# Narrow zero-weight filler matmuls and a scheduler that models tile switches, in a two-layer attention kernel

## The chip, the cores and the metric

The kernel runs on one core of one Trainium2 chip. The metric is the device time of one execution in microseconds. Most executions agree within 0.3%.

In this text ScalarE is ACT, VectorE is DVE and TensorE is PE (PEld for its weight loads) in the profile's lines.

## The reference

Two layers, each of them a multi-query attention (A) followed by a linear attention (B), over 2048 tokens of width 512. A has 32 query heads of width 16 and one head of keys and values:

```python
def _A_ref(x, wq, wk, wv, wo):                       # cut
    q = (x @ wq).reshape(B, S, 32, 16).transpose(0, 2, 1, 3)
    k = x @ wk
    v = x @ wv
    p = softmax(einsum("bhqd,bkd->bhqk", q, k) * 16 ** -0.5)
    o = einsum("bhqk,bkd->bhqd", p, v)
    return o.transpose(0, 2, 1, 3).reshape(B, S, 512) @ wo
...
x = A_x
x = x + A(layernorm(x)); x = x + B(layernorm(x))     # layer 1
x = x + A(layernorm(x)); x = x + B(layernorm(x))     # layer 2
```

What matters is the softmax: 2 x 32 x 2048 x 2048 exponentials. In tiles of 128 keys x 512 (queries, or queries of several heads) these are 4096 score tiles, 2048 for each layer.

## The kernel before

The kernel plans itself. While it is being built, a list scheduler written in Python walks through a model of the engines, with a duration for each operation, and fixes the order of instructions on every engine. On the chip that order is kept, and only semaphores decide when an instruction starts.

A score tile goes one of two ways. ScalarE takes them in threes: three score matmuls, then one exp of 128x1536. VectorE takes them in pairs, with a polynomial in six steps. TensorE then multiplies the tile with the values. Scores use 32 rows of the array (three matmuls in different row groups run side by side), values use 32 columns (four column groups, side by side). Both write to PSUM (TensorE's output memory, eight banks here), of which VectorE's scores and, in the attention stages, all projections share one bank, number 6.

```python
# scores: row group i of 32 rows          (smm, cut)
x = e.matmul(bank(b0 + k), lhsT=Kr[r, m, kt * P:(kt + 1) * P], rhs=QT[r, ..., q0:q0 + n], start=True, stop=True)
# values: column group c of 32 columns    (add_pv, cut)
return e.matmul(ps[32 * c:32 * c + 32, 7 * 512:8 * 512], lhsT=Vaug[:, kt, :], rhs=src, ...)
o = add(PE, 0.1, f, ..., name="pv")
# a projection: four matmuls in two operations of two (proj, cut)
for c in range(0, len(mms), chunk):                  # chunk = 2
    o = add(PE, len(part) * (0.03 + n * 0.36e-3), f, ...)
```

Between these the kernel puts fillers: matmuls with zero weights, added to the bank of the values, so that they change no result. They keep TensorE active enough for its full clock. In the kernel before they use the whole array:

```python
def idle(now):                                       # called when PE has nothing in the model (cut)
    if not sc.order[PE] or streaming(now) > FILL * FILLW:       # 0.6 of the last 1.7 us
        return
    ...
    o = add(PE, 0.03 + FILLN * 0.41e-3, lambda e: e.matmul(bank(7, FILLN), lhsT=zer[:],
            rhs=maskx[:].bitcast(BF16)[:, 0:FILLN], start=not owned, stop=True, ...), prio=9.0, name="dummy")
```

The softmax here doesn't subtract the row's maximum and nothing guards it: scores larger than these inputs give would overflow.

## Time and profile before

| quantity | before |
|---|---|
| time, median | 1781.3 us in 3 runs |
| ScalarE busy | 1728.1 of 1777.9 us, 97% |
| exps (1536 columns each, but for 3 of 1024), one every | 1207, 1.331 us |
| score tiles on VectorE / on ScalarE | 478 / 3618 |
| fillers | 1234 |

The lines of the profile's page, first: span; busy time of the engines; the chain of work that ended last, by engine; then four groups of instructions (line, engine, operation, output<-input, count, busy us and mean ns of one, idle time just before them and what ended it). One record of exp covers about 1.57 us, but the next starts 1.331 us after it, since they overlap.

```profile
span 1777.9 us, 27691 instructions
...
PE 1683.0 (95%) x11642; PEld 533.4 (30%) x11642; DVE 1554.0 (87%) x2767; ACT 1728.1 (97%) x1452; POOL 31.3 (2%) x46
...
ACT 62%; PE 19%; DVE 17%; issue 1%; DMA 0%; POOL 0%; SPq 0%
...
L775 ACT ACTIVATE PTA<-ps_all 128x1536 bf16<-128x1536 f32 x1207 | 1644.0, 1569 | 7.7 <-PE ps_all L635 6.3
...
L897 PE MATMUL ps_all<-maskx,zer 128*128 128x512 bf16 x1234 | 401.0, 386 | 0.0
L829 DVE TENSOR_SCALAR xT<-ps_all 128x512 int32<-128x512 f32 x478 | 327.4, 685 | 80.8 <-PE ps_all L635 78.9
```

Three windows of 100 us in the second attention stage show where the room is. Each line has the start and end, then the busy us and (count) of PE, PEld, DVE, ACT and POOL, the clock, the DMA share and GB/s; two lines are copied, the last window and the sum of the three.

```profile
1600.00:1700.00 100.00, 95.40 (x673) 29.78 (x672) 81.57 (x147) 99.71 (x79) 2.98 (x3) 1.00 0.00 1
sum 300.00, PE 287.33 PEld 86.99 DVE 254.12 ACT 298.49 POOL 5.28; mean PE 95.78 PEld 29.00 DVE 84.71 ACT 99.50 POOL 1.76
```

ScalarE is busy 99.5% of the time there. The timeline of ScalarE shows how tight that is: 24 exps in a row in 32.40 us. From start to start they are 1.331 us apart, but for a few of 1.34 to 1.35 us and one of 1.585 us.

```profile
1098.61 32.40 ACT L775 ACTIVATE PTA<-ps_all 128x1536 bf16<-128x1536 f32 x24
```

So the kernel is a sequence of exps with little between them: 1207 x 1.331 = 1606.5 us of the span of 1777.9 us. The other 171.4 us are called "time outside exps" below. They hold the start (the ramp, before exps follow each other closely), the stretch between the layers, the end, ScalarE's other work, and waits. For waits there is a second number, the "excess": within the two attention stages, how much the distance from each exp to ScalarE's next instruction exceeds 1.331 us, summed. It is 29.3 us before; where exactly a stage is taken to begin and end moves such a sum by about 1 us. (A first version of it, over fixed stretches of time and between neighbouring exps alone, gave 28.7 us before. Some texts quote that one; the tables here use the second.)

The list of waits of VectorE (engine, what waited <- what it waited for: us in total, times, longest):

```profile
DVE xT L829 <- PE ps_all L635: 78.9, 129, 1.3
DVE e_buf L940 <- ACT e_buf L939: 45.2, 29, 2.8
DVE v_tok L958 <- PE ps_all L496: 25.3, 19, 3.1
...
DVE rden L695 <- PE ps_all L692: 2.1, 2, 1.1
```

And a microsecond and a half of TensorE's timeline: scores (line 635), values (671) and a filler (897). Merged lines carry the start of the first matmul of the group.

```profile
401.63 0.39 PE L635 MATMUL ps_all<-QT,Kr 32*128 32x512 bf16 x3
401.95 0.40 PE L671 MATMUL ps_all<-PTA,Vaug 128*32 128x512 bf16 x3
402.28 0.39 PE L897 MATMUL ps_all<-maskx,zer 128*128 128x512 bf16 x1
402.85 0.40 PE L635 MATMUL ps_all<-QT,Kr 32*128 32x512 bf16 x4 [0.18 <-ACT PTA L775]
```

From 401.63 to 401.95 (scores to values) and from 401.95 to 402.28 (values to filler), each change of kind takes 0.32 us from start to start, where two matmuls of one kind in one place take 0.216 us. (The scores at 402.85 had to wait for ScalarE besides.) A change costs about 0.1 us. The Trainium skill, "TensorEngine Tiling (Array Packing)", Key Properties, states that changing the tiling mode drains the engine; this trace agrees and puts a number to it.

### The profile page before, as it was taken

The page shows a single profiled execution, that of the slowest core. Times are in us where ns is not written, and L with a number is a line of the kernel's source. Part 1 is how long each engine was busy: PE and PEld are TensorE (multiplying, and loading weights), DVE is VectorE, ACT ScalarE, POOL GpSimd, SP SyncE. Part 2 cuts the span into 40 slices and gives each one's busy share as a digit, 9 for nine tenths or more (in the row PEclk, how much of TensorE's full clock was granted, in tenths as well). Part 3 has the DMA queues.
Part 4 walks back from the last instruction along what each step waited for, and adds up shares of the span by engine and source line. Part 5 has one row for each costly group of instructions (what it writes and reads, how often), then busy time and mean ns, then how long its engine had stood idle before and what let it go on. Part 6 is the DMA issues. An engine that isn't in the chain of part 4 may idle for free.

```text
span 1777.9 us, 27691 instructions
## 1 busy us (share of the span) xinstructions
PE 1683.0 (95%) x11642; PEld 533.4 (30%) x11642; DVE 1554.0 (87%) x2767; ACT 1728.1 (97%) x1452; POOL 31.3 (2%) x46
## 2 busy tenths in 40 slices
PE   7999999999999999999899999999999999999998
PEld 4222222222232222233442222322222322222334
DVE  7999997999887998878789999879998879978775
ACT  7999999999999999999699999999999999999996
POOL 0000000000000000000000000000000000000000
PEclk9999999999999999999999999999999999999999
DMA  3000000000000000000000000000000000000001
GB/s 120 1 1 1 1 1 1 1 1 1 1 1 1 1 1 1 1 1 1 1 1 1 1 1 1 1 1 1 1 1 1 1 1 1 1 1 1 1 1 48
DMA packets 7724, 9.14 MB, mean 5 GB/s; under 512 B 1456, under 2 KB 7088, under 8 KB 7600
## 3 DMA queue, kind: packets, MB, share of 16 engines
q1 hardware_dynamic: 7600, 7.37, 1.3%
q8 instruction: 91, 1.49, 0.3%
q14 instruction: 33, 0.27, 0.1%
HBM read 5.28 MB, written 2.10 MB: 4 GB/s over the span
## 4 chain that ended last, share of the span: by engine, by line
ACT 62%; PE 19%; DVE 17%; issue 1%; DMA 0%; POOL 0%; SPq 0%
ACT PTA L775 60%; PE ps_all L635 6%; PE ps_all L671 5%; PE ps_all L897 3%; DVE xT L829 3%; DVE PTD L851 3%; PE ps_all L496 2%; ACT e_buf L939 1%; DVE xs L847 1%; DVE xu L846 1%; DVE xs L850 1%; DVE stats L461 1%; PE ps_all L1060 1%; DVE xs L848 1%; DVE xu L849 1%
## 5 line engine op out<-in xcount | busy, mean ns | idle before, releaser
L775 ACT ACTIVATE PTA<-ps_all 128x1536 bf16<-128x1536 f32 x1207 | 1644.0, 1569 | 7.7 <-PE ps_all L635 6.3
L635 PE MATMUL ps_all<-QT,Kr 32*128 32x512 bf16 x4096 | 611.3, 385 | 39.8 <-ACT PTA L775 14.8
L671 PE MATMUL ps_all<-PTA,Vaug 128*32 128x512 bf16 x3618 | 520.1, 390 | 8.2 <-DVE Eo L683 7.8
L897 PE MATMUL ps_all<-maskx,zer 128*128 128x512 bf16 x1234 | 401.0, 386 | 0.0
L829 DVE TENSOR_SCALAR xT<-ps_all 128x512 int32<-128x512 f32 x478 | 327.4, 685 | 80.8 <-PE ps_all L635 78.9
L635 PEld LDWEIGHTS ps_all<-QT,Kr 32*128 32x128 bf16 x4096 | 147.2, 91 | 486.3 <-ACT PTA L775 188.1
L851 DVE SCALAR_TENSOR_TENSOR PTD<-xT,xs 128x1024 uint16<-128x1024 int32 x239 | 290.3, 1215 | 1.8
L671 PEld LDWEIGHTS ps_all<-PTA,Vaug 128*32 128x32 bf16 x3618 | 126.2, 93 | 319.0 <-issue 299.9
L846 DVE TENSOR_SCALAR xu<-xT 128x1024 f16<-128x1024 uint16 x239 | 164.3, 687 | 3.7
L847 DVE TENSOR_TENSOR xs<-xu 128x1024 f16<-128x1024 f16 x239 | 163.5, 684 | 2.9
L850 DVE TENSOR_TENSOR xs<-xs,xu 128x1024 f16<-128x1024 f16 x239 | 163.0, 682 | 2.4
L897 PEld LDWEIGHTS ps_all<-maskx,zer 128*128 128x128 bf16 x1234 | 93.9, 97 | 196.5 <-issue 179.4
L671 PE MATMUL ps_all<-PTD,Vaug 128*32 128x512 bf16 x478 | 128.8, 388 | 18.2 <-DVE Eo L683 11.4
L848 DVE TENSOR_SCALAR xs<-xs 128x1024 f16<-128x1024 f16 x239 | 98.9, 414 | 1.7
L849 DVE TENSOR_SCALAR xu<-xu 128x1024 f16<-128x1024 f16 x239 | 99.2, 415 | 0.0
L496 PE MATMUL ps_all<-wqkv_sb,xnT 128*128 128x512 bf16 x256 | 68.7, 382 | 1.5 <-DVE xT L829 0.9
L940 DVE TENSOR_SCALAR e_buf<-e_buf 128x512 f32<-128x512 f32 x64 | 27.1, 423 | 45.4 <-ACT e_buf L939 45.2
L469 POOL TENSOR_TENSOR rstd<-veps,mhalf 128x1 f32<-128x1 f32 x30 | 27.8, 925 | 1668.5 <-DVE veps L467 1668.5
L939 ACT ACTIVATE e_buf<-ps_all 128x512 f32<-128x512 f32 x64 | 46.0, 719 | 4.8 <-PE ps_all L496 3.1
L671 PEld LDWEIGHTS ps_all<-PTD,Vaug 128*32 128x32 bf16 x478 | 28.2, 93 | 65.2 <-DVE PTD L851 30.7
L461 DVE BATCH_NORM_STATS2 stats<-x_sb 128x6 f32<-128x512 bf16 x64 | 43.2, 680 | 3.8 <-DMA x_sb<-in_A_x_dram 2.9
L683 DVE COPY Eo<-ps_all 128x512 f32<-128x512 f32 x62 | 42.4, 684 | 4.3 <-PE ps_all L671 3.7
(87 smaller groups left out, 825.9 us busy)
## 6 DMA issues: line engine op xcount, KB each, us to landing
out_dram<-x_sb SPq DMA_DIRECT2D x16, 128.0 KB, 1.7
x_sb<-in_A_x_dram SPq DMA_DIRECT2D x3, 512.0 KB, 6.9
wqkv_sb<-in_B_wqkv_dram SPq DMA_DIRECT2D x1, 1536.0 KB, 11.3
x_sb<-in_A_x_dram SPq DMA_DIRECT2D x2, 256.0 KB, 3.1
wq_sb<-in_A_wq_dram SPq DMA_DIRECT2D x1, 512.0 KB, 5.1
wo_sb<-in_A_wo_dram SPq DMA_DIRECT2D x1, 512.0 KB, 8.3
wo_sb<-in_B_wo_dram SPq DMA_DIRECT2D x1, 512.0 KB, 10.9
wk_sb<-in_A_wk_dram SPq DMA_DIRECT2D x1, 16.0 KB, 2.5
```

The lines of the kernel that those rows point to most:

```text
L496: i = e.matmul(bank(h.idx, n), lhsT=l, rhs=r, start=(c + k == 0), stop=(c + k == len(mms) - 1))
L635: x = e.matmul(bank(b0 + k), lhsT=Kr[r, m, kt * P:(kt + 1) * P], rhs=QT[r, self.units[u][0] % 2, gs, q0:q0 + n], start=True, stop=True)
L671: return e.matmul(ps[32 * c:32 * c + 32, 7 * 512:8 * 512], lhsT=Vaug[:, kt, :], rhs=src, start=opened[0], stop=opened[1], skip_group_check ...
L775: oe = add(AC, tac(m * 512), lambda e: e.activation(PTA[:, hp.idx, 0:m * 512], bank(3 * s, m * 512), ACTF.Exp, scale=SCALE), deps=[o] + pr ...
L829: o = add(DV, tdv(512), lambda e: e.tensor_scalar(out=xT[:, hx.idx, i * 512:(i + 1) * 512], in0=bank(6), scalar1=SCALE * LOG2E * 65536.0, ...
L846: o = add(DV, tdv(w, 0.52), lambda e: e.tensor_scalar(out=u_, in0=lo, scalar1=1.0 / 65536, scalar2=-0.5, op0=ALU.mult, op1=ALU.add), deps= ...
L847: o1 = add(DV, tdv(w, 0.52), lambda e: e.tensor_tensor(out=s_, in0=u_, in1=u_, op=ALU.mult), deps=[o] + c["prev"], name="xsq", **kw)
L848: o2 = add(DV, tdv(w, 0.26), lambda e: e.tensor_scalar(out=s_, in0=s_, scalar1=XK, scalar2=-XW, op0=ALU.mult, op1=ALU.add), deps=[o1], nam ...
L849: o3 = add(DV, tdv(w, 0.26), lambda e: e.tensor_scalar(out=u_, in0=u_, scalar1=1.0, scalar2=XL, op0=ALU.mult, op1=ALU.add), deps=[o1], nam ...
L850: o4 = add(DV, tdv(w, 0.52), lambda e: e.tensor_tensor(out=s_, in0=s_, in1=u_, op=ALU.mult), deps=[o2, o3], name="xc", **kw)
L851: o5 = add(DV, tdv(w), lambda e: e.scalar_tensor_tensor(out=PTD[:, hp.idx, 0:w].bitcast(U16), in0=xT[:, k, 0:w], scalar=2.0 ** -9, in1=s_, ...
L897: o = add(PE, 0.03 + FILLN * 0.41e-3, lambda e: e.matmul(bank(7, FILLN), lhsT=zer[:], rhs=maskx[:].bitcast(BF16)[:, 0:FILLN], start=not ow ...
```

## The change

The intent: let a filler queue behind the last value matmul, in the same mode and the same column group, so that no switch is paid and values of other column groups can run beside it. Further, tell the scheduler's model what the trace shows (a pass of 512 columns is 0.217 us, a switch 0.1 us, transposes and projections are shorter than it thought), and hold matmuls back that would run into a more urgent one. The part "no bank lent" is no edit: that option was already off.

The diff, cut to its core:

```diff
+SWITCH, PASS = 0.1, 0.217
...
+    def pe_need(self, o):                 # when may o start on PE, by kind (F full, S scores, P values)
+        k, g = o.pk
+        if k != self.pk:
+            return self.pend_t + SWITCH
+        return self.pend_t if k == "F" else max([self.pgrp.get(x, 0.0) for x in g])
...
+            if e == PE:                   # in the loop over ready operations, most urgent first
+                need = self.pe_need(o)
+                if need > self.now + 1e-9:
+                    if limit is None or need < limit:
+                        limit = need
+                        self.at(need, None)
+                    continue
+                if limit is not None and self.now + o.dur[PE] > limit + 0.03:
+                    continue              # the "reserving rule" of the text below
...
-    FILL, FILLW, FILLN = 0.6, 1.7, 512
+    AWIN, ATGT, ATGT2 = 1.7, 0.5, 0.6
...
-            o = add(PE, len(part) * (0.03 + n * 0.36e-3), f, ...)    # and eight more such durations
+            o = add(PE, len(part) * (0.006 + n * 0.42e-3), f, ...)
...
-            o = add(PE, 0.1, f, ..., name="pv")
+            o = add(PE, PASS, f, pk=("P", (c,)), ..., name="pv")
...
+            twice = not self.ramp and not owned and activity(sc.now) < ATGT2 and sc.tfree[AC] > sc.now + 3 * PASS
+                if twice:
+                    self.smm(e, got, 3 * s)          # scores computed twice, as a filler between units
...
+            c = max(range(4), key=lambda c: sc.pgrp.get(c, 0.0) if sc.pk == "P" else 0.0)
+            f = lambda e: e.matmul(ps[32 * c:32 * c + 32, 7 * 512:8 * 512], lhsT=zer[:, 0:32],
+                                   rhs=maskx[:].bitcast(BF16)[:, 0:512], start=not owned, stop=True, ...)
```

More of the change, by code (lines that the diff above doesn't have):

```diff
@@ L17 @@
 FLEX = 0.0
+SWITCH, PASS = 0.1, 0.217
 class Op:
     __slots__ = ("engs", "fn", "dur", "prio", "deps", "nleft", "succ", "rt", "guard", "acq", "uses", "rel", "cb",
-                 "eng", "t0", "vis", "idx", "gidx", "waits", "marked", "val", "vc", "dma", "done", "name")
+                 "eng", "t0", "vis", "idx", "pk", "gidx", "waits", "marked", "val", "vc", "dma", "done", "name")
 class Holder:
@@ L64, in __init__ @@
         self.idle = lambda now: None
+        self.pk, self.pgrp, self.pend_t = "F", {}, 0.0
     def add(self, engs, dur, fn, reads=(), writes=(), prio=5.0, guard=None, acq=(), uses=(), rel=(), cb=None, deps=(),
-            dma=False, name=""):
+            dma=False, name="", pk=("F", ())):
         o = Op()
+        o.pk = pk
         o.engs = engs if isinstance(engs, tuple) else (engs,)
@@ L128, in _try @@
             cand = sorted(ready, key=lambda r: (r[0] + (FLEX if len(r[2].engs) > 1 and self.act_ok(r[2]) else 0.0), r[1]))
+        limit = None
         for i, (p, s, o) in enumerate(cand):
@@ L167, in _start @@
         end = self.now + o.dur[e]
+        if e == PE:
+            if o.pk[0] != self.pk:
+                self.pk, self.pgrp = o.pk[0], {}
+            for x in o.pk[1]:
+                self.pgrp[x] = end
+            self.pend_t = max(self.pend_t, end)
         o.vis = end + (3.0 if o.dma else LAT[e])
-        self.tfree[e] = end
-        self.at(end, None)
+        self.tfree[e] = end if e != PE or o.pk[0] == "F" else self.now + 0.004
+        self.at(self.tfree[e], None)
         self.at(o.vis, None)
@@ L480, in tr @@
             return i
-        o = add(PE, 0.45, tr, reads=["ident"], deps=[o], uses=[hx], acq=[hb], rel=[hx], prio=prio, name="tr")
+        o = add(PE, 0.22, tr, reads=["ident"], deps=[o], uses=[hx], acq=[hb], rel=[hx], prio=prio, name="tr")
         def cp(e):
@@ L498, in proj @@
             kw = dict(acq=[h]) if c == 0 else dict(uses=[h], deps=[o])
-            o = add(PE, len(part) * (0.03 + n * 0.36e-3), f, reads=reads, prio=prio, name=name, **kw)
+            o = add(PE, len(part) * (0.006 + n * 0.42e-3), f, reads=reads, prio=prio, name=name, **kw)
         return o
@@ L527, in f @@
             return k
-        o = add(PE, 0.16 * n, f, reads=["wv"] + [("xnT", t) for t in range(t0, t0 + n)], acq=[h], prio=prio, name="vp")
+        o = add(PE, 0.1 * n, f, reads=["wv"] + [("xnT", t) for t in range(t0, t0 + n)], acq=[h], prio=prio, name="vp")
         def ev(e):
@@ L558, in q_tile @@
             kw = dict(acq=[h]) if c == 0 else dict(uses=[h], deps=[o])
-            o = add(PE, 0.55, f, reads=["wq", ("xnT", t)], prio=prio, name="qt", **kw)
+            o = add(PE, 0.445, f, reads=["wq", ("xnT", t)], prio=prio, name="qt", **kw)
         def ev(e):
@@ L667, in cb @@
                     self.norm(u, o)
+            c = (j % NRG) * (4 // NRG) + j // NRG
             def f(e):
-                c = (j % NRG) * (4 // NRG) + j // NRG
                 return e.matmul(ps[32 * c:32 * c + 32, 7 * 512:8 * 512], lhsT=Vaug[:, kt, :], rhs=src, start=opened[0], stop=opened[1],
                                 skip_group_check=True)
-            o = add(PE, 0.1, f, reads=[("V", kt)], deps=[dep], uses=[hold], rel=[hold] if last else [], prio=2.0 + 1e-4 * u, guard=guard, cb=cb, name="pv")
+            o = add(PE, PASS, f, pk=("P", (c,)), reads=[("V", kt)], deps=[dep], uses=[hold], rel=[hold] if last else [], prio=2.0 + 1e-4 * u, guard=guard, cb=cb, name="pv")
             return o
@@ L693, in tr @@
                 return i
-            o = add(PE, 1.0, tr, reads=["identf"], deps=[oe], acq=[ht, hos] if par == 0 else [ht], uses=[he], rel=[he], prio=1.2, name="trA")
+            o = add(PE, 0.48, tr, reads=["identf"], deps=[oe], acq=[ht, hos] if par == 0 else [ht], uses=[he], rel=[he], prio=1.2, name="trA")
             o = add(DV, 0.168, lambda e: e.reciprocal(rden[:, hr.idx, :].unsqueeze(2), bank(ht.idx).rearrange("p (a c) -> p a c", c=32)[:, :, DH:DH + 1]),
@@ L766, in fill @@
             m = len(got)
+            u = self.acc_owner
+            owned = u >= 0 and 0 < sum(self.count[u]) < 64
+            twice = not self.ramp and not owned and activity(sc.now) < ATGT2 and sc.tfree[AC] > sc.now + 3 * PASS
             def f(e):
+                if twice:
+                    self.smm(e, got, 3 * s)
                 return self.smm(e, got, 3 * s)
-            o = add(PE, 0.2 + 0.014 * m if RG == 32 else 0.05 + 0.14 * m, f, reads=self.keys(got), deps=prev, uses=[h], prio=0.0, name="sA")
+            o = add(PE, PASS * (-(-m * RG // P)) * (2 if twice else 1), f, reads=self.keys(got), deps=prev, uses=[h], prio=0.0, name="sA",
+                    pk=("S", tuple(dict.fromkeys(self.parts(q)[0] for q in got))))
             hp = Holder(p_pta)
@@ L827, in dstep @@
             banks.hist[6] = []
-            o = add(PE, 0.22, lambda e: self.smm(e, [p], 6), reads=self.keys([p]), deps=prev, uses=[h], prio=1.5, name="sD")
+            o = add(PE, PASS, lambda e: self.smm(e, [p], 6), reads=self.keys([p]), deps=prev, uses=[h], prio=1.5, name="sD", pk=("S", (self.parts(p)[0],)))
             o = add(DV, tdv(512), lambda e: e.tensor_scalar(out=xT[:, hx.idx, i * 512:(i + 1) * 512], in0=bank(6), scalar1=SCALE * LOG2E * 65536.0,
@@ L874, in bass_interleave_layers__grouped_kv_mqa__linear_attn_block__prompt_kernel, with activity @@
     sc.step = ctl.step
-    def streaming(now):
-        tot = 0.0
+    def activity(now):
+        tot, first = 0.0, now
         for o in reversed(sc.order[PE]):
-            if o.t0 + 1.5 < now - FILLW:
+            if o.t0 + 1.5 < now - AWIN:
                 break
-            st = {"pv": 0.071, "sA": 0.2 if RG == 32 else 0.4, "dummy": 0.2}.get(o.name, 0.85 * o.dur[PE])
-            end = o.t0 + o.dur[PE]
-            if end > now - FILLW:
-                tot += st * min(1.0, (end - (now - FILLW)) / o.dur[PE])
-        return tot
+            a, b = max(o.t0, now - AWIN), min(o.t0 + o.dur[PE], now)
+            if o.pk[0] == "P":
+                b = min(b, first)
+                first = min(first, o.t0)
+            if b > a:
+                tot += (b - a) * (RG / P * len(o.pk[1]) if o.pk[0] == "S" else 0.95)
+        return tot / AWIN
     def idle(now):
-        if not sc.order[PE] or streaming(now) > FILL * FILLW:
+        if not sc.order[PE] or any(not d.done or d.vis > now for d in (sc.lastw["mask"], sc.lastw["zer"])):
             return
@@ L892, in idle @@
         owned = u >= 0 and 0 < sum(ctl.count[u]) < 64
-        if not owned and not banks.free[7]:
+        if not owned and (not banks.free[7] or any(d.vis > now for d in banks.hist[7])):
             return
-        if owned and now < sc.tfree[AC] < now + 0.1:
+        if activity(now) > ATGT:
             return
-        o = add(PE, 0.03 + FILLN * 0.41e-3, lambda e: e.matmul(bank(7, FILLN), lhsT=zer[:], rhs=maskx[:].bitcast(BF16)[:, 0:FILLN], start=not owned, stop=True, skip_group_check=True),
-                reads=["mask", "zer"], deps=[] if owned else list(banks.hist[7]), prio=9.0, name="dummy")
+        kind = "F" if sc.pk == "F" else "P"
+        need = sc.pend_t + (0.0 if sc.pk == kind else SWITCH)
+        if need > now + 1e-9:
+            sc.at(need, None)
+            return
+        if any(not o.done and not o.acq and (o.guard is None or o.guard()) for (_, _, o) in sc.ready[PE]):
+            return
+        if owned and now < sc.tfree[AC] + LAT[AC] < now + PASS + SWITCH:
+            return
+        if kind == "F":
+            f = lambda e: e.matmul(bank(7), lhsT=zer[:], rhs=maskx[:].bitcast(BF16)[:, 0:512], start=not owned, stop=True, skip_group_check=True)
+            pk = ("F", ())
+        else:
+            c = max(range(4), key=lambda c: sc.pgrp.get(c, 0.0) if sc.pk == "P" else 0.0)
+            f = lambda e: e.matmul(ps[32 * c:32 * c + 32, 7 * 512:8 * 512], lhsT=zer[:, 0:32], rhs=maskx[:].bitcast(BF16)[:, 0:512],
+                                   start=not owned, stop=True, skip_group_check=True)
+            pk = ("P", (c,))
+        o = add(PE, PASS, f, reads=["mask", "zer"], deps=[] if owned else list(banks.hist[7]), prio=9.0, name="dummy", pk=pk)
         banks.hist[7].append(o)
-        sc._try(PE)
+        sc._start(PE, o)
     sc.idle = idle
@@ L916, in tr @@
             return i
-        o = add(PE, 0.45, tr, reads=["ident", ("Osb", g % 2, 0), ("Osb", g % 2, 1)], acq=[h], uses=[hos], rel=[hos], writes=keys, prio=pr, name="otr")
+        o = add(PE, 0.22, tr, reads=["ident", ("Osb", g % 2, 0), ("Osb", g % 2, 1)], acq=[h], uses=[hos], rel=[hos], writes=keys, prio=pr, name="otr")
         def cp(e):
@@ L985, in pq_tile @@
             kw = dict(acq=[h]) if g == 0 else dict(uses=[h], deps=[o])
-            o = add(PE, 0.27, f, reads=["wqkv", ("xnT", t)], prio=pr, name="pq", **kw)
+            o = add(PE, 0.224, f, reads=["wqkv", ("xnT", t)], prio=pr, name="pq", **kw)
         phi(h, o, pqT[:, :, ts], [("pq", g, t) for g in range(NG)], 2.4, tiled=True)
@@ L1006, in kv_block @@
                 rd = [t] if i > 0 else tl
-                o = add(PE, 0.22, f, reads=[(k, tt) for k in ("pk", "vB") for tt in rd], prio=3.4, name="kv", **kw)
+                o = add(PE, 0.172, f, reads=[(k, tt) for k in ("pk", "vB") for tt in rd], prio=3.4, name="kv", **kw)
             dst = kvacc if b == 0 else kvtmp
@@ L1050, in den @@
             return i
-        o = add(PE, 0.3, den, reads=[("zb", g) for g in range(NG)] + [("pq", g, t) for g in range(NG)], acq=[win, hd], prio=pr - 0.4, name="den")
+        o = add(PE, 0.223, den, reads=[("zb", g) for g in range(NG)] + [("pq", g, t) for g in range(NG)], acq=[win, hd], prio=pr - 0.4, name="den")
         o = add(AC, tac(512), lambda e: e.activation(e_buf[:, he.idx, :], bank(hd.idx), ACTF.Ln, bias=1e-6), deps=[o], uses=[hd], acq=[he], rel=[hd], prio=0.4 + 0.01 * t, name="ln")
```

## The prediction

> **What bounds the kernel now.** ScalarE. The page's first part has ACT busy 1728.1 of 1777.9 us (97%), PE 95%, DVE 87%; the chain of waits gives ACT 62%, PE 19%, DVE 17%. The table of windows has ACT at 99.3 to 100% in nearly every 100 us of the two attention stages (34 to 848 and 913 to 1731 us). The timeline shows exps of 128x1536 starting every 1.331 us back to back; 1207 of them are about 1606 us. Summed over neighbouring exps of both stages, their distance exceeds 1.331 us by 12 + 16 = 29 us: all that a quicker TensorE could return to ScalarE directly. Outside lie 34 us of start, 65 us between the layers and 47 us of end, made of latency chains.
>
> VectorE takes 478 of the 4096 score tiles; a pair costs it about 5.47 us (groups of lines 829 to 851) and saves ScalarE 2/3 of an exp, 0.89 us. It idles some 160 us in the attention stages; the list of waits puts 78.9 us on the score matmul, 45 on the phi exp, 25 on the v projection.
>
> **What the change does.**
> 1. Today 1234 zero-weight 128x128 matmuls sit between scores (32-row tiles) and values (32-column tiles). Starts are 0.31 to 0.32 us apart across a change of kind, 0.216 us within one: a change costs 0.1 us. The Trainium skill, "TensorEngine Tiling (Array Packing)", Key Properties, says that changing the tiling mode drains the engine; the trace agrees. A filler in the last value's column group removes the values-to-filler change (some 650, about 65 us of TensorE time), and values of other groups can run beside it.
> 2. The model now holds 0.217 us passes and 0.1 us changes, which match the trace; no filler starts when a ready matmul could; shorter projections and transposes change the order.
> 3. Fillers follow a different activity measure: target 0.5 instead of 0.6. I expect about as many, 1000 to 1500, plus some doubled scores between units.
> 4. "No bank lent" is already so before.
>
> **Clock.** The windows show two throttled stretches of 3.4 us (mean clock 0.998). The Trainium skill, "TensorE: Matmul & The Clock Gate", Part 1, ties the clock to activity over about 3.4 us; both come just after windows among the lowest in activity when values count by rows, not columns. So 32-column fillers should hold the clock; that is inferred, not shown.
>
> **On the critical path.** Little: TensorE time saved is slack for ScalarE. I give 8 us of the 29 back, 2 us from ramp and tail, and about 20 us less DVE waiting for scores, worth some 4 pairs, 4 us. Total 14 us.
>
> Predicted: 1767 us, 8 times in 10 between 1749 and 1784. Faster by over 2%: 0.08; within 2%: 0.88; slower: 0.04.
>
> **What would show it.** Right: exps still 1.331 us back to back, ACT near 97%; excess between exps 15 to 25 us; values-to-filler starts 0.216 us apart; DVE tiles 480 to 500; DVE's wait for scores 50 to 70 us; clock at least 0.99. Step 1 is wrong if such pairs still take 0.31 us; the clock step, if throttled stretches grow beyond a few.
>
> **What would make it wrong.** The throttle counts columns: scores and values double in length and ScalarE starves. Fillers delay the next value or score so that exps wait more. Or VectorE takes many more tiles, or the transitions shorten (to 1745 or below). The new order alone moves the time some us either way.

## The result, and the profile after

The changed kernel takes 1774.97 us (median of 4 runs, 1773.49 to 1775.08), the kernel before 1781.56 us in the same rounds. The ratio is 0.9963, with a 95% interval from 0.9945 to 0.998. Ratios here are the mean time of one kernel's runs over that of the other's runs of the same rounds, so not quite the ratio of the medians quoted. The change is real and small: 6.6 us between the medians, where 14 us had been forecast. The time itself lies inside the forecast range.

The same lines of the page after:

```profile
span 1773.2 us, 27569 instructions
...
PE 1598.6 (90%) x11542; PEld 508.4 (29%) x11655; DVE 1526.3 (86%) x2724; ACT 1726.5 (97%) x1457; POOL 32.0 (2%) x46
...
ACT 91%; PE 4%; DVE 4%; DMA 0%; issue 0%; SPq 0%; ACTq 0%
...
L809 ACT ACTIVATE PTA<-ps_all 128x1536 bf16<-128x1536 f32 x1211 | 1653.9, 1836 | 2.6 <-PE ps_all L661 2.4
...
L863 DVE TENSOR_SCALAR xT<-ps_all 128x512 int32<-128x512 f32 x466 | 319.2, 685 | 66.0 <-PE ps_all L661 64.4
L947 PE MATMUL ps_all<-maskx,zer 128*32 128x512 bf16 x1043 | 333.1, 382 | 0.0
```

The chain of waits went from 62% to 91% ScalarE, and TensorE's share in it from 19% to 4%: TensorE has stopped setting the pace almost everywhere. (Its busy time is partly lower because some matmul records are missing: 11542 matmuls against 11655 weight loads.) But the exps went from 1207 to 1211, and VectorE's tiles from 478 to 466, against the forecast of 480 to 500.

The windows of the same stretch:

```profile
1600.00:1700.00 100.00, 90.93 (x655) 28.62 (x660) 76.31 (x132) 100.00 (x80) 3.38 (x3) 1.00 0.00 1
sum 300.00, PE 271.23 PEld 83.05 DVE 252.98 ACT 300.00 POOL 6.44; mean PE 90.41 PEld 27.68 DVE 84.33 ACT 100.00 POOL 2.15
```

ScalarE is at 100.00 of 100 us. In the timeline of TensorE the filler (line 947, now 128x32 weights) follows the values (698) after 0.23 us from the start of their group, and no longer after 0.33 us:

```profile
402.33 0.39 PE L661 MATMUL ps_all<-QT,Kr 32*128 32x512 bf16 x3
402.65 0.40 PE L698 MATMUL ps_all<-PTA,Vaug 128*32 128x512 bf16 x3
402.88 0.59 PE L947 MATMUL ps_all<-maskx,zer 128*32 128x512 bf16 x2
403.51 0.39 PE L661 MATMUL ps_all<-QT,Kr 32*128 32x512 bf16 x3
```

VectorE's waits:

```profile
DVE xT L863 <- PE ps_all L661: 64.4, 120, 1.2
DVE e_buf L992 <- ACT e_buf L991: 58.6, 23, 4.1
DVE v_tok L1010 <- PE ps_all L522: 27.6, 15, 3.1
DVE rden L722 <- PE ps_all L719: 13.7, 13, 1.7
```

The wait for scores fell as forecast, from 78.9 to 64.4 us. Other waits of VectorE rose: for the exp of phi (the feature map of B) from 45.2 to 58.6, for the transposed output from 2.1 to 13.7.

Where the time of the profiled run went, worked out from the starts of the exps in the two traces:

| part | before, us | after, us |
|---|---|---|
| exps x 1.331 | 1606.5 | 1611.8 |
| outside exps: up to the 25th exp | 22.0 | 21.9 |
| rest of the first attention stage | 26.2 | 23.1 |
| between the layers, up to the 25th exp of the second | 50.6 | 52.3 |
| rest of the second attention stage | 30.7 | 20.6 |
| after the last exp | 41.9 | 43.4 |
| sum outside exps | 171.4 | 161.4 |
| excess (part of the above) | 29.3 | 17.3 |

ScalarE got 13 us back in the attention stages. Of these, 5.3 us went into four more exps and about 3 us into a longer stretch between the layers and a longer end. This table is the puzzle for the experiments: was it the filler's form that gave 13 us, and what took away VectorE's tiles?

### The profile page after: what moved, and what is told of

The parts are those of the page before. It is cut to its first block, busy times and chain, and to the rows that moved or that the text cites. A ratio compares the mean times of both kernels' runs of the same rounds, so it can differ in the third digit from the quotient of the medians. Undisturbed runs are those within 1.5% of the kernel's fastest.

```text
span 1773.2 us, 27569 instructions
## 1 busy us (share of the span) xinstructions
PE 1598.6 (90%) x11542; PEld 508.4 (29%) x11655; DVE 1526.3 (86%) x2724; ACT 1726.5 (97%) x1457; POOL 32.0 (2%) x46
## 4 chain that ended last, share of the span: by engine, by line
ACT 91%; PE 4%; DVE 4%; DMA 0%; issue 0%; SPq 0%; ACTq 0%
ACT PTA L809 89%; ACT e_buf L991 2%; PE ps_all L1112 1%; DVE stats L487 1%; PE ps_all L522 1%; DVE xn_buf L498 0%; DVE Kr L537 0%; PE ps_all L698 0%; PE ps_all L661 0%; DMA x_sb<-in_A_x_dram 0%; DVE xnT L511 0%; PE ps_all L1110 0%; DVE pqT L1106 0%; PE ps_all L1101 0%; PE ps_all L943 0%; ACT e_buf L1104 0%
## 5 line engine op out<-in xcount | busy, mean ns | idle before, releaser
L863 DVE TENSOR_SCALAR xT<-ps_all 128x512 int32<-128x512 f32 x466 | 319.2, 685 | 66.0 <-PE ps_all L661 64.4
L947 PE MATMUL ps_all<-maskx,zer 128*32 128x512 bf16 x1043 | 333.1, 382 | 0.0
L885 DVE SCALAR_TENSOR_TENSOR PTD<-xT,xs 128x1024 uint16<-128x1024 int32 (+1 forms) x234 | 283.4, 1211 | 1.8
L880 DVE TENSOR_SCALAR xu<-xT 128x1024 f16<-128x1024 uint16 (+1 forms) x234 | 160.1, 684 | 3.4
L881 DVE TENSOR_TENSOR xs<-xu 128x1024 f16<-128x1024 f16 (+1 forms) x234 | 159.6, 683 | 3.0
L884 DVE TENSOR_TENSOR xs<-xs,xu 128x1024 f16<-128x1024 f16 (+1 forms) x234 | 158.9, 679 | 2.3
L947 PEld LDWEIGHTS ps_all<-maskx,zer 128*32 128x32 bf16 x1043 | 93.4, 96 | 86.1 <-issue 45.0
L882 DVE TENSOR_SCALAR xs<-xs 128x1024 f16<-128x1024 f16 (+1 forms) x234 | 97.0, 415 | 2.5
L883 DVE TENSOR_SCALAR xu<-xu 128x1024 f16<-128x1024 f16 (+1 forms) x234 | 97.2, 416 | 0.0
L992 DVE TENSOR_SCALAR e_buf<-e_buf 128x512 f32<-128x512 f32 x64 | 27.0, 422 | 59.0 <-ACT e_buf L991 58.6
L991 ACT ACTIVATE e_buf<-ps_all 128x512 f32<-128x512 f32 x64 | 60.3, 942 | 6.8 <-PE ps_all L1035 3.4
L1010 DVE CAST v_tok<-ps_all 128x512 bf16<-128x512 f32 x32 | 22.0, 688 | 30.2 <-PE ps_all L522 27.6
```

Of the source, the lines that this page charges most:

```text
L863: o = add(DV, tdv(512), lambda e: e.tensor_scalar(out=xT[:, hx.idx, i * 512:(i + 1) * 512], in0=bank(6), scalar1=SCALE * LOG2E * 65536.0, ...
L880: o = add(DV, tdv(w, 0.52), lambda e: e.tensor_scalar(out=u_, in0=lo, scalar1=1.0 / 65536, scalar2=-0.5, op0=ALU.mult, op1=ALU.add), deps= ...
L881: o1 = add(DV, tdv(w, 0.52), lambda e: e.tensor_tensor(out=s_, in0=u_, in1=u_, op=ALU.mult), deps=[o] + c["prev"], name="xsq", **kw)
L882: o2 = add(DV, tdv(w, 0.26), lambda e: e.tensor_scalar(out=s_, in0=s_, scalar1=XK, scalar2=-XW, op0=ALU.mult, op1=ALU.add), deps=[o1], nam ...
L883: o3 = add(DV, tdv(w, 0.26), lambda e: e.tensor_scalar(out=u_, in0=u_, scalar1=1.0, scalar2=XL, op0=ALU.mult, op1=ALU.add), deps=[o1], nam ...
L884: o4 = add(DV, tdv(w, 0.52), lambda e: e.tensor_tensor(out=s_, in0=s_, in1=u_, op=ALU.mult), deps=[o2, o3], name="xc", **kw)
```

## The experiments

Before a kernel ran, its plan could be counted: number of exps, of VectorE tiles and of fillers are fixed when it is built. Those counts are in the expectations. Twelve kernels ran, in three sets of four; all gave correct results. Kernels of one set share 11 runs of the kernel before (medians 1780.3, 1780.6 and 1778.8 us), and each set ran on another chip; so between sets the ratios are compared, or runs of equal clock.

| run | VectorE tiles | exps | outside exps, us | excess, us | median, us | ratio to before, 95% interval | granted clock of its runs |
|---|---|---|---|---|---|---|---|
| before | 478 | 1207 | 171.4 | 29.3 | about 1780 | 1 | 0.995 to 1.0 |
| after | 466 | 1211 | 161.4 | 17.3 | 1775.0 | 0.9963 (0.9945 to 0.998) | 0.997 to 1.0 |
| e1_wide_fillers | 466 | 1211 | 169.0 | 21.0 | 1778.4 | 0.999 (0.9977 to 1.0003) | 0.994 to 0.998 |
| e2_no_reserve | 485 | 1204 | 171.0 | 19.5 | 1773.3 | 0.9966 (0.9953 to 0.9978) | 0.994 to 0.998 |
| e3_before_short | 490 | 1203 | 180.7 | 34.7 | 1784.4 | 1.0047 (1.0015 to 1.008) | 0.986 to 0.998 |
| e4_no_fillers | 488 | 1203 | 292.6 | 135.6 | 1895.5 | 1.0653 (1.0638 to 1.0669) | 0.779 to 0.787 |
| e5_reserve_ramps | 489 | 1203 | 165.7 | 19.8 | 1767.9 | 0.9929 (0.9915 to 0.9942) | 0.996 to 0.999 |
| e6_fewer_dve | 434 | 1222 | 163.6 | 17.0 | 1792.1 | 1.0076 (1.0055 to 1.0097) | 0.988 to 0.998 |
| e7_before_narrow | 478 | 1207 | 165.4 | 21.9 | 1773.3 | 0.9967 (0.9952 to 0.9982) | 0.992 to 0.997 |
| e8_switch_free | 492 | 1202 | 175.6 | 28.9 | 1780.3 | 1.0008 (0.9994 to 1.0022) | 0.992 to 0.999 |
| e9_reserve_not_proj | 483 | 1206 | 164.6 | 19.4 | 1772.1 | 0.9966 (0.9951 to 0.9981) | 0.989 to 0.997 |
| e10_old_durations | 460 | 1214 | 163.1 | 15.2 | 1780.4 | 1.001 (0.9997 to 1.0023) | 0.997 to 0.999 |
| e11_no_doubles | 487 | 1204 | 163.6 | 16.2 | 1766.3 | 0.9929 (0.9918 to 0.9941) | 0.998 to 1.0 |
| e12_fewer_fillers | 491 | 1202 | 167.9 | 22.9 | 1768.8 | 0.9945 (0.9932 to 0.9957) | 0.987 to 0.995 |

"Outside exps" and "excess" are of the one profiled run, with whatever its clock cost it. That run of e1 was the slowest of its five (1782.6 us at a clock of 0.994; the other four 1777.8 to 1779.4), and that of e8 the fastest of its six (1777.3 at 0.999).

The clock column matters for reading small differences. Over the 33 runs of the kernel before in the three sets, those with a mean clock of 1.0 took 1778.4 us (11 runs) and those with 0.997 took 1781.05 us (5 runs); a straight line through all gives 1.0 us for each 0.001. A throttled stretch in the records lasts 3.413 us or a multiple of it, at half clock, and 3.413 us of it lower the mean of such a run by about 0.001. So, as an estimate from that line, one throttled stretch of that length costs about 1 us, and two runs of the same kernel differ mainly by how many they caught (the line accounts for 81% of the variance of these 33 runs).

### e1: the new order with wide fillers

```diff
@@
-            f = lambda e: e.matmul(ps[32 * c:32 * c + 32, 7 * 512:8 * 512], lhsT=zer[:, 0:32], rhs=maskx[:].bitcast(BF16)[:, 0:512],
+            f = lambda e: e.matmul(bank(7), lhsT=zer[:], rhs=maskx[:].bitcast(BF16)[:, 0:512],
```

> The changed kernel with every instruction in the same order; only the 1043 narrow fillers are written 128 columns wide again. Theory A (the narrow form itself returned the ScalarE waits): a values-to-filler distance goes back from 0.216-0.226 us to 0.31-0.32 us, the summed excess of neighbouring exps over 1.331 us in the two attention stages goes from 15.7 us back to 25 us or more, and the time rises by 8 to 15 us to about 1785 us. Rival B (the new order and model did it, the form is slack): the distance rises all the same, the excess stays under 20 us and the time stays within 3 us of 1775 us.

The distance from values to filler went back: with the same order, the median distance between the weight loads of a value and of the filler after it is 0.320 us here and 0.015 us in the changed kernel. The time came out between the two expectations: 1778.4 us, 3.4 us above the changed kernel by medians, with an excess of 21.0 us. Theory A's size was too large, rival B's too small. In the new order the narrow form is worth some 3 us. At a clock of 0.998, which three of its runs had, it took 1777.8 to 1778.4 us, where the changed kernel had 1775 us at 0.997; so the difference isn't the clock's. (The profiled run, from which 169.0 and 21.0 us are, is not typical: it has 20.5 us of throttled time, two stretches of it between the layers, where the changed kernel's has 10.2 us.)

### e7: the old order with narrow fillers

This is the opposite test, run in the second set. Every instruction keeps its place in the old order; 1012 of the 1234 fillers directly follow a value matmul (or such a filler) and become narrow.

```diff
@@
+            self.colof = {}
@@
+            self.colof[id(o)] = (j % NRG) * (4 // NRG) + j // NRG
@@
-        o = add(PE, 0.03 + FILLN * 0.41e-3, lambda e: e.matmul(bank(7, FILLN), lhsT=zer[:], rhs=maskx[:].bitcast(BF16)[:, 0:FILLN], start=not owned, stop=True, skip_group_check=True),
+        me = []
+
+        def f(e):
+            c = ctl.colof.get(id(sc.order[PE][me[0].idx - 1]))
+            if c is None or me[0].idx == 0:
+                return e.matmul(bank(7, FILLN), lhsT=zer[:], rhs=maskx[:].bitcast(BF16)[:, 0:FILLN], start=not owned, stop=True, skip_group_check=True)
+            ctl.colof[id(me[0])] = c
+            return e.matmul(ps[32 * c:32 * c + 32, 7 * 512:8 * 512], lhsT=zer[:, 0:32], rhs=maskx[:].bitcast(BF16)[:, 0:512], start=not owned, stop=True, skip_group_check=True)
+        o = add(PE, 0.03 + FILLN * 0.41e-3, f,
@@
+        me.append(o)
```

> The kernel before, every instruction in its old order; only fillers that directly follow a value matmul or another narrow filler are written 32 columns wide in that value's column group. 1207 exps as before. The opposite test to the wide fillers in the new order, which cost about 3 us. If the narrow form is worth the same in the old order: 1776 to 1778 us where the kernel before takes 1779 to 1780, and the excess of neighbouring exps falls from 29 to about 25 us. If the form is worth more where the order was made without it: 1770 to 1774 us. If nothing: 1779 us or more.

```profile
span 1771.9 us, 27691 instructions
...
ACT 79%; DVE 12%; PE 8%; issue 1%; DMA 0%; SPq 0%
...
L831 DVE TENSOR_SCALAR xT<-ps_all 128x512 int32<-128x512 f32 x478 | 327.3, 685 | 76.4 <-PE ps_all L636 74.8
...
L906 PE MATMUL ps_all<-maskx,zer 128*32 128x512 bf16 x1012 | 320.4, 379 | 0.0
```

1773.3 us, inside the expectation "worth more where the order was made without it". The median distance from a value matmul to the filler after it fell from 0.322 to 0.226 us, over the same 624 pairs. The same 478 tiles and 1207 exps as before; the excess fell from 29.3 to 21.9 us, the time outside exps from 171.4 to 165.4. The ratio of 0.9967 cannot be told from the changed kernel's 0.9963. So the fillers' form alone, with nothing else of the change, gives as much as the whole change. Everything else in it, the model of switches, the reserving rule, the new durations, the doubled scores, comes to nothing on top of that. At a clock of 0.997 it seems even to have cost 1 to 3 us: four runs of e7 took 1772.1 to 1773.7 us there, two of the changed kernel, in other rounds, 1775.0 us. What follows asks why: whether these parts do nothing, or do good and harm.

### e2: without the reserving rule

```diff
@@
-                if limit is not None and self.now + o.dur[PE] > limit + 0.03:
+                if False:
```

> The changed kernel without the rule by which the model leaves TensorE idle rather than start a matmul that would run past the earliest start of a more urgent one of another kind. VectorE then gets 485 score tiles instead of 466 and ScalarE 1204 exps instead of 1211. Theory C (the time missing from my forecast went into the 12 tiles that moved from VectorE to ScalarE, and this rule moved them): 7 exps fewer are 9.3 us, so about 1766 us, with the excess of neighbouring exps below 20 us. Rival D (the rule is what keeps the urgent scores on time): the excess rises by 8 us or more and eats the gain, 1772 to 1780 us.

VectorE got 485 tiles and ScalarE 7 exps fewer, and the time was still 1773.3 us, not 1766. Neither expectation is met as written (the time is in rival D's range, the excess is not). The 9.3 us of the exps are gone and 9.6 us outside exps have come (161.4 to 171.0). But the excess accounts only for 2.2 of them. Taken apart like the table above, 1.8 us are in the first ramp, 4.5 between the layers up to the 25th exp, 3.6 in the rest of the second attention stage; the other two parts cancel. Some of this is the clock: the profiled run of e2 has 17.1 us of throttled time, with one stretch between the layers and two in the second attention stage, and that of the changed kernel has 10.2 us, all in the first attention stage. At about 1 us for each 3.4 us, the throttling is about 2 us of the 9.6 us, and about 1 us of the 4.5 and 2 us of the 3.6 us. So the rule may do harm in one place and good in another, which is what e5 tries.

### e5: the rule in the ramps only

```diff
@@
+        self.reserve = lambda: True
@@
-                if limit is not None and self.now + o.dur[PE] > limit + 0.03:
+                if self.reserve() and limit is not None and self.now + o.dur[PE] > limit + 0.03:
@@
+    sc.reserve = lambda: ctl.ramp or ctl.tail
```

> The changed kernel with the reserving rule kept only in the ramps and between the layers, and dropped in the attention stages: 489 VectorE tiles, 1203 exps (the changed kernel: 466 and 1211; without the rule at all: 485 and 1204). Without the rule at all, 7 exps fewer (9.3 us) gave almost nothing, since the time that ScalarE is not in exps rose by 9.6 us in the profiles, 6.3 of them in ramp and transition. Theory G (the rule is needed in the ramps and only costs tiles in the stages): the time outside exps goes back towards 161 to 165 us and the kernel takes 1764 to 1769 us. Rival H (the rule protects scores in the stages, and what looked like the ramp was chance of the order): outside exps 169 us or more, 1771 us or more.

Theory G holds: 1767.9 us, inside its range, with 165.7 us outside exps (its range ended at 165). The ramp and the stretch between the layers are back to what the changed kernel has, to 0.1 us each (22.0 and 52.4 us). One plan doesn't prove that the rule alone did it: e11 below, with the same rule in the ramps, has 22.9 and 54.3 us there (one throttled stretch). This version beats both kernels: 0.9929 of before, against 0.9963.

How the rule took VectorE's tiles is seen in the projections. A projection is two operations of two matmuls. TensorE's timeline of the changed kernel, with scores (661), values (698), fillers (947) and one projection (522):

```profile
506.11 0.40 PE L698 MATMUL ps_all<-PTA,Vaug 128*32 128x512 bf16 x3
506.34 0.59 PE L947 MATMUL ps_all<-maskx,zer 128*32 128x512 bf16 x2
506.87 0.60 PE L522 MATMUL ps_all<-wqkv_sb,xnT 128*128 128x512 bf16 x2
507.40 0.39 PE L661 MATMUL ps_all<-QT,Kr 32*128 32x512 bf16 x3
507.73 0.40 PE L698 MATMUL ps_all<-PTA,Vaug 128*32 128x512 bf16 x3
508.05 0.61 PE L522 MATMUL ps_all<-wqkv_sb,xnT 128*128 128x512 bf16 x2
```

The first half of the projection runs at 506.87, the second only at 508.05: it would have run into the more urgent scores, so the rule held it back. All that time the projection holds the bank that it shares with VectorE's scores. In e5 the four matmuls stay together (line 523):

```profile
301.77 0.39 PE L662 MATMUL ps_all<-QT,Kr 32*128 32x512 bf16 x3
302.10 1.04 PE L523 MATMUL ps_all<-xnT,wq_sb 128*128 128x512 bf16 x4
303.07 0.39 PE L662 MATMUL ps_all<-QT,Kr 32*128 32x512 bf16 x3
303.39 0.40 PE L699 MATMUL ps_all<-PTA,Vaug 128*32 128x512 bf16 x3
```

Over the 130 projections with 512 columns of the attention stages, the time from the first to the last weight load of a projection sums to 85 us before (32 of them over 1 us), 121 us after (66), 59 us in e5 and 58 us in e2 (none). VectorE got 478, 466, 489 and 485 tiles. That the held bank is the link between the two is argued, and splitting alone doesn't fix the number: e8 (the rule kept, but no cost of a switch) has 47 such projections and 492 tiles, and e4 (the rule kept, no fillers) has 58 that are split and 488 tiles. What took the tiles is the rule in a model that also has the switch and the fillers.

### e9: the rule in the stages for scores and values, not for projections

Against e5:

```diff
@@
-                if self.reserve() and limit is not None and self.now + o.dur[PE] > limit + 0.03:
+                if limit is not None and (self.reserve() or o.pk[0] != "F") and self.now + o.dur[PE] > limit + 0.03:
```

> As the kernel that reserves in the ramps only (489 VectorE tiles, 1203 exps, 1767.9 us), but in the attention stages the rule holds for scores and values too, and not for projections and transposes: 483 tiles, 1206 exps. Theory J (what cost VectorE tiles was that the rule split projections, so that they held their bank longer; for scores and values it shortens waits): the time from the first to the last weight load of a projection stays near 0.45 us, the excess of neighbouring exps falls from 19.8 us to 16 to 18 us, and the time is 1767 to 1770 us, since 3 exps more cost 4 us. Rival K (the rule protects nothing in the stages): excess 20 us or more, 1771 us or more.

In the stages the rule now spares all work on the whole array, that is projections and transposes. The projections stay together (59 us in sum, none over 1 us) and VectorE has 483 tiles instead of 466, so it was the rule's hold on this work that split the projections and cost most of the tiles. The rest of theory J fails: the excess is 19.4 us, as good as e5's 19.8, and the time is 1772.1 us. Rival K's time is met. With 3 exps more than e5 and nothing gained by waits, the rule in the attention stages is not worth having in either form. (Part of the 4 us to e5 is the clock, 0.989 to 0.997.)

### e6: the price of a VectorE tile

```diff
@@
-            if self.dcur is None and self.pa + LEAD + 2 >= n:
+            if self.dcur is None and (self.pa + LEAD + 2 >= n or 600 <= self.pa < 760):
```

> The changed kernel with VectorE barred from starting pairs in one stretch of each layer: 434 VectorE tiles instead of 466, 1222 exps instead of 1211. It prices the tiles. If ScalarE's exps are the time, 11 exps more are 14.6 us: 1788 to 1791 us, all of it in the attention stages. If part of it is hidden (VectorE and TensorE then have room, fewer waits), less: 1780 to 1786 us.

32 tiles fewer and 11 exps more, with no other edit: 1792.1 us by the median. In the profiled runs the span rose from 1773.2 to 1790.1 us, 16.9 us, of which 14.6 are the exps and 2.2 lie outside them. The first expectation holds (its range ended 1 us below). None of a tile's price is hidden: 0.44 us each, two thirds of 1.331 us for a pair. With that, the 12 tiles that the change lost are 5.3 us, and the 8 that the forecast had gained would have been 3.5 us.

### e8: no cost of a switch in the model

```diff
@@
-SWITCH, PASS = 0.1, 0.217
+SWITCH, PASS = 0.0, 0.217
```

> The changed kernel with the cost of a tile switch in the model set from 0.1 us to 0: 492 VectorE tiles, 1202 exps, 9 fewer than in the changed kernel (12 us). If the switch in the model is what makes the plan one that TensorE can keep, the excess of neighbouring exps rises from 17 us to 28 us or more and the time is 1773 us or more; if the switch in the model only makes it shy of giving tiles to VectorE, the excess stays below 20 us and the time is 1763 to 1767 us.

492 tiles, the most of all, and 1780.3 us, no better than before. The excess went from 17.3 to 28.9 us and the time outside exps from 161.4 to 175.6. The first theory holds: a plan made without switches gives VectorE more tiles, but TensorE can't keep it, and ScalarE waits longer. So the switch in the model saves 14 us outside exps and costs 12 us in exps. Tiles alone don't make a kernel fast; e5 has 489 of them with 19.8 us of excess.

### e3 and e10: the durations of projections and transposes

In e3 the kernel before gets only the new durations; in e10 the changed kernel gets the old ones back.

```diff
@@
-        o = add(PE, 0.45, tr, reads=["ident"], deps=[o], uses=[hx], acq=[hb], rel=[hx], prio=prio, name="tr")
+        o = add(PE, 0.22, tr, reads=["ident"], deps=[o], uses=[hx], acq=[hb], rel=[hx], prio=prio, name="tr")
@@
-            o = add(PE, len(part) * (0.03 + n * 0.36e-3), f, reads=reads, prio=prio, name=name, **kw)
+            o = add(PE, len(part) * (0.006 + n * 0.42e-3), f, reads=reads, prio=prio, name=name, **kw)
... (seven more durations, each as in the change)
```

> The kernel before, with only the model's durations of projections and transposes changed as in the change (0.45 to 0.22 us and so on); wide fillers, no model of tile switches. VectorE gets 490 tiles, ScalarE 1203 exps: 4 exps fewer than before are 5.3 us. If the number of exps tells the time and the excess stays at 29 us: about 1776 us. If too short a model puts work on TensorE that it can't do, the excess rises above 35 us and the time is 1781 us or more. The model itself says nothing here of which.

```diff
@@
-        o = add(PE, 0.22, tr, reads=["ident"], deps=[o], uses=[hx], acq=[hb], rel=[hx], prio=prio, name="tr")
+        o = add(PE, 0.45, tr, reads=["ident"], deps=[o], uses=[hx], acq=[hb], rel=[hx], prio=prio, name="tr")
@@
-            o = add(PE, len(part) * (0.006 + n * 0.42e-3), f, reads=reads, prio=prio, name=name, **kw)
+            o = add(PE, len(part) * (0.03 + n * 0.36e-3), f, reads=reads, prio=prio, name=name, **kw)
... (seven more durations, each put back in the same way)
```

> The changed kernel with the model's durations of projections and transposes put back as they were before: 460 VectorE tiles, 1214 exps, 3 more than in the changed kernel (4 us). If the shorter durations only moved that number: 1778 to 1780 us where the changed kernel takes about 1774. If plans made with the long durations are also worse in the transitions: 1782 us or more. If the long durations are safer (fewer waits): 1775 us or less.

In the old model the shorter durations gain nothing: 490 tiles, but the excess rises from 29.3 to 34.7 us, the clock drops to 0.986 and 0.987 in two runs, and the time is 1784.4 us (the second expectation, whose 35 us of excess are just missed). Much of the loss is the clock: its two runs at 0.997 and 0.998 took 1781.5 and 1780.9 us, where the kernel before took 1780.3 to 1781.6 us. So 4 exps fewer bought nothing, and the lower clock came on top. That model has no switches, and its long transposes stood in for them to some degree; that last is an argument, not a measurement. In the new model going back to long durations costs 3 exps (4.0 us) and 1.7 us outside exps in the profile: 1780.4 us, 0.4 us above the range of the first expectation. So the same edit is worth some 5 us in the new model and nothing in the old one.

### e4, e11 and e12: fillers, doubled scores and the clock

```diff
@@
-    sc.idle = idle
```

> The changed kernel without any filler (1203 exps, 488 VectorE tiles; 52 doubled scores stay). Theory E (fillers hold the clock and cost little): the mean granted clock falls well below 0.95, passes double where it does, the excess rises above 40 us, and the time is 1790 us or more. Rival F (values and scores alone hold the clock, or ScalarE doesn't feel a slower TensorE): 1770 us or less.

```profile
PEclk9777569656999776888797577887759896679797
...
ACT 46%; PE 38%; DVE 14%; issue 1%; DMA 0%; POOL 0%; SPq 0%
```

Theory E. Without fillers the clock is 0.78 in the mean, and TensorE is 38% of the chain of waits. Against the changed kernel the time outside exps rises by 131 us. The Trainium skill, "TensorE: Matmul & The Clock Gate", Part 1, states that the clock follows activity over windows of about 3.4 us, and its table has two states, half and full clock. The traces agree: the throttled stretches in the profiles of the kernel before and of the changed one last 3.413 us, one of them twice that (6.827 us), all at half clock. In the changed kernel 1043 of the fillers are 32 columns wide, and its clock is 0.997 to 1.0; with wide ones in the same order (e1) it is 0.994 to 0.998. In the old order it is the other way round: narrow fillers (e7) had 0.992 to 0.997, wide ones (the kernel before, same rounds) 0.995 to 1.0. A filler of 32 columns thus holds the clock about as well as one of 128 here, within some 0.002.

The other two are variants of e5. First without doubled scores, then with a lower target for the activity:

```diff
@@
-            twice = not self.ramp and not owned and activity(sc.now) < ATGT2 and sc.tfree[AC] > sc.now + 3 * PASS
+            twice = False
```

> The kernel that reserves in the ramps only, without doubled scores (34 there, none here): 487 tiles, 1204 exps. Theory L (doubled scores hold the clock where no filler may go, between units): the granted clock falls from 0.996-0.999 to 0.99 or lower, and at about 1.1 us for each throttled stretch of 3.4 us the time is 1773 us or more. Rival M (they do nothing): 1767 to 1770 us, clock as before.

```diff
@@
-    AWIN, ATGT, ATGT2 = 1.7, 0.5, 0.6
+    AWIN, ATGT, ATGT2 = 1.7, 0.4, 0.6
```

> The kernel that reserves in the ramps only, with the filler target lowered from 0.5 to 0.4: 717 fillers instead of 1204, 491 tiles, 1202 exps. Without any filler the clock was 0.78 and the time 1895 us. If 0.5 holds a margin that isn't needed: clock 0.99 or more, 1763 to 1767 us, the fastest here. If the target is where it has to be: clock below 0.98, some 15 or more throttled stretches, 1775 us or more.

Doubled scores do nothing that shows: 1766.3 us without them, clock 0.998 to 1.0, rival M (0.7 us below its range). With 717 fillers instead of 1204 the clock sits at 0.987 to 0.995, and 1768.8 us is no gain over e5 although two tiles were won. It lies between the two expectations. Its two runs at 0.994 and 0.995 took 1766.0 and 1766.5 us, so the lower clock eats what the plan had gained. A target of 0.4 is no better than 0.5; others weren't tried.

## Why the prediction was right or wrong

**Right.** ScalarE bounds the kernel; exps stay 1.331 us apart; TensorE's saved time is mostly slack. The filler no longer pays the switch after values (0.32 to 0.22 us from start to start). There are 1127 fillers, of the forecast 1000 to 1500, and 40 times three doubled scores. The clock holds, as the prediction had inferred from two windows of the trace. That inference was weak: in the trace of the kernel before, both windows are among the four lowest of 497 whether values count by rows or by columns (worked out from the starts of its matmuls, each taken as 0.216 us). What speaks against a count by columns is e1, where four times the columns in 1043 fillers gave no better clock. VectorE's wait for scores is 64.4 us, in the range of 50 to 70.

**Wrong in size: "I give 8 us of the 29 back".** It was 12 us (29.3 to 17.3). The form of the fillers alone gave 7.4 us in the old order (e7).

**Wrong in sign, and the step that failed: "about 20 us less DVE waiting for scores, worth some 4 pairs, 4 us".** The waiting did fall by 14.5 us, and the pairs fell by 6. The inference from one to the other was false. How many tiles VectorE gets isn't decided on the chip by whether it waits; it is decided by the model while the kernel is built. To know that number one had to ask what each edit does to the model's VectorE, and there the reserving rule, which the prediction doesn't name (it has only that no filler starts when a ready matmul could, another line of the diff), splits projections and holds bank 6 longer. Without it the plan has 485 tiles, with it 466; with it, but spared for work on the whole array in the stages, 483 (e9). It needs the rest of the model to do so: without the cost of a switch the plan has 492 tiles with the rule in place (e8). In time that is 5.3 us lost where 4 us were to be won, a miss of 9.3 us.

**Wrong in sign, small: "2 us from ramp and tail".** The stretch between the layers grew by 1.7 us and the end by 1.5 us. No run was aimed at why.

Put together for the profiled runs: 13.2 us won in the two attention stages, 5.3 us lost to four more exps, 3.2 us lost between and after the layers, 0.1 us won at the start, which makes 4.8 us; the spans differ by 4.7 us, the medians of all runs by 6.6 (the profiled run of the kernel before was its fastest). Against the forecast of 14 us, 9.2 us are missing: 9.3 by the tiles and 5.1 by ramp and ends, while the waits gave 5.2 us more than was said. That the time fell inside the forecast range says little: the range of 1749 to 1784 us would have held no change at all, too.

**The warning that came true** was the last one: "the new order alone moves the time some us either way". It had been treated as noise; the change in the number of exps alone is 5.3 us, nearly as much as the whole gain of 6.6 us.

**Left open.** Why the order without the rule makes the ramp and the stretch between the layers longer by some 6 us (about 1 us of it by a throttled stretch) was not taken further; the opposite of e5, with the rule in the attention stages only, was built and not run (466 tiles by its plan). The profiles give one run each, so differences of 1 or 2 us in "outside exps" are not firm.

## What to carry to other kernels

If a build-time scheduler decides who does the work, read a change of its model as a change of work: count what each engine gets in the new plan, and price that count, before costing any wait. An instruction that exists only to keep a clock up should have the tile mode and the place of the work before it; this one edit alone gave as much as the whole change here. And a rule that keeps the pipe free for urgent work should be asked what the held-back work is itself holding.

## What the Trainium skill lacked or had wrong

- "TensorEngine Tiling (Array Packing)", Key Properties, says that a change of mode drains the engine, without a cost. Here a change between 32-row, 32-column and full mode costs about 0.1 us from start to start (0.32 against 0.216 us for 512 columns).
- "TensorE: Matmul & The Clock Gate", Part 1, doesn't say whether activity goes by rows, columns or time. Zero-weight fillers of 32 columns held the clock at 0.997 to 1.0 where the same order with 128 columns had 0.994 to 0.998; in the old order it was 0.992 to 0.997 with 1012 of them narrow, 0.995 to 1.0 with all wide.
- The same page, Terms, prices throttled time at that time x (1 - K/N), K/N being the granted share; for a 3.4 us stretch at half clock that is an estimate of 1.7 us. It has no figure for a kernel bound by another engine: here, bound by ScalarE, a stretch cost about 1 us (the line over 33 runs).
- "ScalarE: Activation LUTs", What ACT_TABLE_LOAD costs, gives 186 ns + 0.833 ns for each column for an ACTIVATE with immediate scale and bias, and an overlap of about 93 ns back to back. An exp of 1536 columns by itself shows 1.451 us here, which agrees (an estimate by the page's formula is 1.466 us), but back to back they start 1.331 us apart, an overlap of 120 ns.
